# Pooled attention feeding a top-1 mixture of experts: a hold in GpSimd's queue, the pace of three routings and eight weight pieces moved

## The chip, the cores and the metric

The kernel runs on one core of a Trainium2 chip. The metric is the device time of one execution in microseconds (us), as a median over several runs. The core has five engines that each work through a queue of their own in order and wait for each other by semaphores: TensorE (PE; its weight loads are listed as PEld), VectorE (DVE), ScalarE (ACT), GpSimd (POOL) and SyncE (SP), which only issues DMAs here. ACT and GpSimd issue DMAs too.

## What is computed

Attention over keys and values that are averaged in groups of 8 positions, then a mixture of experts in which each row goes to one expert, up to a capacity:

```python
def _attn_ref(q, k, v):              # batch 8, heads 8, seq 576, head_dim 64
    k_p = k.reshape(B, H, Sp, pool, D).mean(axis=3)
    v_p = v.reshape(B, H, Sp, pool, D).mean(axis=3)
    scores = scale * np.matmul(q, k_p.transpose(0, 1, 3, 2))
    scores = scores - np.max(scores, axis=-1, keepdims=True)
    attn = np.exp(scores)
    attn = attn / (np.sum(attn, axis=-1, keepdims=True) + 1e-09)
    return np.matmul(attn, v_p)

def _moe_ref(x, w_gate, w1, w2, capacity):   # x: 4608 rows of 512; 8 experts, hidden 1024
    logits = x @ w_gate
    expert_idx = np.argmax(logits, axis=1)
    ...
    for i in range(N):
        e = expert_idx[i]
        if counts[e] < capacity:
            disp[e, counts[e]] = x[i]
            ...
    h = np.maximum(np.einsum('ecd,edf->ecf', disp, w1), 0.0)
    y = np.einsum('ecf,efd->ecd', h, w2)
    ...
            out[i] = gate_w[i] * y[expert_idx[i], pos[i]]
```

## The kernel before

It has two parts. The attention part takes about the first third of the span, and a loop over tiles of rows of one expert takes the rest. The change touches the attention part alone.

**Units.** The work of the attention is cut into 36 units of 128 rows of queries (line 688): four for each of the 8 batch entries, and one more for each pair of entries, which holds the tails of both. Lines 1029 to 1090 are one Python loop over units n = 0 to 37 that emits the instructions. All engines' orders follow from it, since nothing is scheduled later. In round n unit n gets its scores (`ps`), its maximum (`mx`) and the subtraction (`pt`), unit n+1 its transposed queries (`pq`, copied to `qT` by ACT), and unit n−2 its transposed probabilities (`pp`, copied to `pT` by ACT in two halves), its product with the values (`pa`, line 516, in two halves) and its normalization on DVE (`rz`, `xo`, `lt`, lines 525 to 542). There is one buffer `pa`, so TensorE can begin the next unit's `pa` when `lt` is done.

**Two banks.** The transposes of `pp`, `pq`, `pk` (pooled keys or values), the products `pv` and the routing's sums `po` take turns in two PSUM banks (`bank`, line 247). Each takes the bank of the last but one, and so waits until that one has been read.

**Pooling.** The keys and values of two batch entries (a pair) are summed over 8 positions by trees of three additions on GpSimd (`tree`, lines 365 to 377: L370, L372, L374), six trees a pair. A queue of generators, `gq`, holds these steps, and each round takes some of them (line 1088). `pooled` and `pool` put a pair's trees into the queue. In the rounds of pair 1 a copy to `apart` that reads the newest `mx` (L1019) goes ahead of the fourth pair's trees, so that GpSimd starts them only when DVE has got that far.

**Routing.** When a pair's logits are there, `route` (lines 584 to 686) finds each row's expert and place: `gmx`, `gd` (L598), `gme`, `gmm`, the one-hot `oh` (L614, L617), counts within a block `su` (L621) and `cum` (L628) on DVE, then the sums over partitions and blocks `po` on TensorE (L641), then the places (L644 to L672) on DVE, and at last scatters of row numbers and weights to the table `slots` in DRAM by GpSimd (L679), queued in `sq`. It is a generator, and each `yield` ends a step. A round takes steps of it at several places: one behind `mx`, some behind `pa` (line 1078), and one behind each of three instructions of the normalization. Between L628 and `po` it yields three times when it has more than three groups. `slots` is first filled with defaults by a DMA of the SP queue (L339), which `setup_rows` issues in round 12.

**Early weights.** From round 25 on the first expert's `w1` is loaded into buffers of the pooling. Eight pieces of it are split (L125 on ACT, L126 on GpSimd) into a high part `w1h` and a low part `w1l`, as steps of `gq`: two at the end of each of rounds 26, 27, 30 and 31. `masks` (lines 343 to 347) makes masks from the capacity on DVE in round 27. In round 29 a gather fetches the first rows `xg`, which are transposed in rounds 31 and 32 (`pxe`).

Of the kernel before, what the change touches and what calls it, by code (L numbers as in the profile page):

```python
# [31 lines left out]
def pooled_attn_top1_moe(ctx: ExitStack, tc: tile.TileContext, q, k, v, wg, w1, w2, cap, out):  # L32
# [7 lines left out]
    nc = tc.nc  # L40
# [51 lines left out]
    def gather(dst, ix, src):  # L92
        nc.gpsimd.tensor_sub(guard[:, :, 0:1], ix[:, :, 0:1], ix[:, :, 0:1])  # L93
        for i in range(2):
            nc.gpsimd.indirect_dma_start(out=dst[:, i, :].bitcast(F32), out_offset=None, in_=src,  # L95
                                         in_offset=bass.IndirectOffsetOnAxis(ap=ix[:, i, 0:1], axis=0))
# [65 lines left out]
    with ExitStack() as actx:  # L162
# [10 lines left out]
        def bank(shape, name, dtype=F32):  # L173

            turn[0] ^= 1
            return ptp.tile(shape, dtype, name=name, tag=f"tp{turn[0]}")
# [17 lines left out]
        def load_kv(p):  # L194
            raws[p] = [[early_k if p == 1 and src is k and i == 0 else load_third(src, p, i) for i in range(3)] for src in (k, v)]
# [142 lines left out]
        def setup_rows():  # L338
            nc.sync.dma_start(slots.rearrange("(p c) t -> p c t", p=P), ids[:, 0:NCOL, :])  # L339
            nc.sync.dma_start(xs[NT : NT + 1, :], zrow[0:1])  # L340
            nc.sync.dma_start(capt, cap.bitcast(I32).rearrange("(o c) -> o c", o=1).to_broadcast([P, 2]))
# [11 lines left out]
        apart = ac.tile([P, 1], F32, name="apart")  # L353
# [25 lines left out]
        def red(dst, t):  # L379
            nc.vector.tensor_reduce(out=dst, in_=t.rearrange("p c (j d) -> p c d j", j=POOL), axis=AX.X, op=ALU.add)  # L380

        def pooled(p):

            kps[p] = kvp.tile([P, NR, D], F32, name="kp", tag="kp", bufs=2)
            vps[p] = kvp.tile([P, NR, D], F32, name="vp", tag="vp", bufs=2)
# [181 lines left out]
        first, lgs, rows_out, early = {}, {}, [], {}  # L567

        def flush():
            while rows_out:  # L570
                nc.scalar.dma_start(*rows_out.pop(0))
# [12 lines left out]
        def route(bp, t0, G, blk, tail, prods, sc, count=False, run=None):  # L584
# [7 lines left out]
            f, nb, n = blk  # L592
            bs = slice(f, f + nb * n)
            mx = sm.tile([P, G, 1], F32, name="gmx", tag="gmx")
# [35 lines left out]
            if gn > 3:  # L630
                yield
                yield
                yield
            po = bank([P, 512], "po")[:, 0 : 4 * E].rearrange("p (a e) -> p a e", a=4)
            prods = [x for x in prods if before or x[1] != "c"]
            for n_, (w, x, l, m) in enumerate(prods):
# [60 lines left out]
        rq, hq, aq, dq, sq, gq = [], [], [], [], [], []  # L697
# [26 lines left out]
        def step(q_, n=1):  # L724

            while q_ and n:
                if callable(q_[0]):
                    q_.pop(0)()
                    n -= 1
                elif next(q_[0], 0) == 0:  # L730
                    q_.pop(0)
                else:
                    n -= 1

        def drain(q_):
            while q_:
                step(q_)

        with tc.manual_schedule():
# [26 lines left out]
            nu = len(units)  # L766
            n_start = nu - 3
            early_b = B // 2
            n_early = nu - 11
# [68 lines left out]
            def start_rows():  # L838
                early["x"] = wk.tile([P, 2, DM], F32R, name="xg", tag="xg", bufs=1)
                idp = early["id"]  # L840
                gather(early["x"], idp, xs[0 : early_b * S, :])
# [141 lines left out]
            NPU = 2 * NB + 1  # L983
# [21 lines left out]
            def hooks(n):  # L1005

                p, j = divmod(n, NPU)
                if n == 0:
                    red(vps[0][:, NR - 1 :], raws[0][1][2][:, 2:3])
                    pooled(1)  # L1010
                    pool(1)
                if p == B // 2:
                    return
                if p + 2 < B // 2:
                    if j == (4 if p == 0 else 2):
                        load_kv(p + 2)
                    if j == (7 if p == 0 else 5):
                        if p:
                            nc.gpsimd.tensor_copy(apart, early["mx"][:, 0, 0:1])  # L1019
                        pooled(p + 2)  # L1020
                        pool(p + 2)
                if n == 3 * NB:
                    drain(gq)
                    gq.append(setup_rest())
                    drain(gq)
                    setup_rows()

            for n in range(nu + 2):
                u = units[n] if n < nu else None
                p = units[n - 2] if n > 1 else None  # L1030
                nx = units[n + 1] if n + 1 < nu else None
                new = n and u and u.b != units[n - 1].b
                if new:
                    assert not aq
                    ahead(u.b)
                if n == n_start:
                    start_weights()
                if n == n_early:
                    start_early()
                if n == n_early + 1:  # L1040
                    drain(gq)
                    split_early(0, 2 * KD, nc.gpsimd)
                if n == n_early + 3:
                    start_ids()
                if n == n_early + 4:
                    start_rows()
                if u:
                    u.score(0)
                if p:
                    p.p_t(0)  # L1050
                if u:
                    u.score(1)
                    u.softmax()
                step(aq)
                if p:
                    p.p_t(1)
                if n == nu + 1:
                    for c in range(KF):
                        nc.scalar.copy(wr["h"][:, c], wr[2][:, c])
                if n >= nu:  # L1060
                    hidden(0, n - nu)
                if nx:
                    nx.q_part()
                flush()
                step(aq)
                if n == 1:
                    busy(5)
                    hq.append(prep_v(0))
                    step(hq)
                if u:  # L1070
                    u.exp()
                if p:
                    p.open()
                    p.av(0)
                turns(n)
                if p:
                    p.av(1)
                step(rq, 4 if NPU < n < nu - 8 else 8 if n >= nu - 8 else 0)
                step(dq)
                if p:  # L1080
                    p.norm()
                    r = route_of(p)
                    if r:
                        rq.append(r)
                        if p.b == early_b - 1:
                            rq.append(favourite())
                hooks(n)
                step(gq, 4 if n <= n_early else 0 if n_early + 3 <= n < n_early + 5 else 2)
                step(sq, 2 if n < nu - 10 else 4)
                step(aq)  # L1090
            flush()
# [132 lines left out]
```

## Time and profile before

| | |
|---|---|
| median of 3 runs | 639.11 us (638.94 to 639.9) |
| the profiled execution | 639.53 us, of which its span 637.5 us |
| mean granted TensorE clock | 0.987 |
| attention part | to about 185 us of the span |
| loop over tiles | from about 216 us on |

The profile lists instructions by engine and line, with tiles by the names above (out<-in). A timeline row has the start and the length in us, the engine, line, operation, tiles, shapes, the number of merged instructions, and in brackets the idle time of the engine just before, with what ended it. "pa L516 <- DVE lt L542" in the list of waits is TensorE's wait before `pa` for DVE's `lt`. A windows row has the stretch, its length, the busy time of an engine (with its instructions), the granted clock, the DMA share and GB/s. The granted clock is 1.00 at full speed.

### The profile page before, as it was taken

The numbers are of one execution on the slowest core, as the hardware profiler recorded it, in microseconds if no ns is written. First come the engines' busy times: TensorE is split into PE (matmuls) and PEld (weight loads), VectorE is DVE, ScalarE is ACT, GpSimd is POOL, SyncE is SP. The second block draws the span as 40 slices with busy tenths as digits, with TensorE's granted clock in tenths as the row PEclk, the third lists the DMA queues.
The fourth block names the chain that finished last, engine by engine and source line by source line (L and its number), as shares of the span: only waits on it lengthen the run. The fifth ranks groups of instructions, "written<-read, shape, count | busy, mean of one in ns | idle before, by whom it ended". The sixth has DMA issues, their size and how long they took to land.

```text
span 637.5 us, 14824 instructions
## 1 busy us (share of the span) xinstructions
PE 614.1 (96%) x4249; PEld 554.1 (87%) x4250; DVE 332.5 (52%) x720; ACT 236.3 (37%) x403; POOL 297.4 (47%) x468
## 2 busy tenths in 40 slices
PE   9899999899999999999899999999999999999994
PEld 8889899798889889988789989988899888989983
DVE  4667868777788322268447731326422585323222
ACT  2555576366544211157245511117111472111111
POOL 7799499253743422424435522434434145441344
PEclk9999999799999999999999999999999999999997
DMA  9989953283191610228728640213612181210112
GB/s 325 359 330 323 349 183 122 72 258 101 53 329 53 230 35 33 66 81 309 241 82 308 230 141 33 66 33 120 235 47 66 41 282 36 66 51 19 62 49 66
DMA packets 47084, 93.81 MB, mean 147 GB/s; under 512 B 13392, under 2 KB 23632, under 8 KB 47060
## 3 DMA queue, kind: packets, MB, share of 16 engines
q1 hardware_dynamic: 30836, 60.37, 27.6%
q0 software_dynamic: 11392, 21.57, 11.3%
q10 hardware_dynamic: 4832, 11.56, 4.8%
q8 instruction: 14, 0.23, 0.1%
q14 instruction: 10, 0.08, 0.0%
HBM read 132.97 MB, written 31.27 MB: 258 GB/s over the span
## 4 chain that ended last, share of the span: by engine, by line
PE 60%; DVEq 2%; issue 2%; DVE 1%; POOL 1%; ACT 0%; POOLq 0%; ACTq 0%
PE y L159 30%; PE ph L150 23%; PE ph L1140 4%; PE px L1117 2%; PE ph L1147 1%; DVE w2l L126 0%; POOL out_dram L100 0%; DVE hl L1130 0%; DVEq L1165 0%; DVEq L1164 0%; DVEq L1163 0%; ACT w2h L125 0%; DVEq L1160 0%; DVEq L1159 0%; POOL xg L95 0%
## 5 line engine op out<-in xcount | busy, mean ns | idle before, releaser
L1129 ACT ACTIVATE hh<-ph 128x512 fp32r<-128x512 f32 x60 | 35.8, 598 | 170.1 <-PE ph L150 170.0
L1130 DVE SCALAR_TENSOR_TENSOR hl<-ph,hh 128x512 fp32r<-128x512 f32 x60 | 40.7, 690 | 109.4 <-ACT hh L1129 62.5
L150 PE MATMUL ph<-xh,w1h 128*128 128x256 f32 x480 | 76.5, 282 | 4.6 <-DVE hl L1130 3.9
L150 PE MATMUL ph<-xh,w1l 128*128 128x256 f32 x480 | 75.9, 281 | 0.0
L150 PE MATMUL ph<-xl,w1h 128*128 128x256 f32 x480 | 75.9, 281 | 0.0
L150 PEld LDWEIGHTS ph<-xh,w1h 128*128 128x128 f32 x480 | 65.8, 189 | 6.9 <-DVE hl L1130 4.8
L159 PE MATMUL y<-w2h,hh 128*128 128x512 f32 x280 | 71.7, 398 | 0.0
L95 POOL DMA_INDIRECT xg<-xs,ix x42 | 43.5, 1035 | 58.2 <-PE y L159 50.0
L516 PE MATMUL pa<-vbd,pT 96*128 96x146 f32 (+1 forms) x480 | 67.1, 296 | 3.5 <-DVE lt L542 3.5
L159 PE MATMUL y<-w2h,hl 128*128 128x512 f32 x280 | 69.3, 390 | 0.0
L159 PE MATMUL y<-w2l,hh 128*128 128x512 f32 x280 | 69.2, 389 | 0.0
L150 PEld LDWEIGHTS ph<-xl,w1h 128*128 128x128 f32 x480 | 65.2, 190 | 0.0
L150 PEld LDWEIGHTS ph<-xh,w1l 128*128 128x128 f32 x480 | 64.7, 189 | 0.0
L516 PEld LDWEIGHTS pa<-vbd,pT 96*128 96x128 f32 (+1 forms) x480 | 57.1, 181 | 6.8 <-DVE lt L542 4.5
L159 PEld LDWEIGHTS y<-w2l,hh 128*128 128x128 f32 x280 | 52.6, 188 | 11.1
L159 PEld LDWEIGHTS y<-w2h,hl 128*128 128x128 f32 x280 | 52.6, 188 | 10.9
L100 POOL DMA_INDIRECT out_dram<-zrow,iz x40 | 51.3, 1282 | 16.9 <-issue 14.9
L159 PEld LDWEIGHTS y<-w2h,hh 128*128 128x128 f32 x280 | 49.6, 188 | 9.6 <-ACT hh L125 0.9
L126 DVE TENSOR_TENSOR xl<-px,xh 128x512 fp32r<-128x512 f32 x40 | 25.8, 686 | 60.9 <-ACT xh L125 60.9
L93 POOL TENSOR_TENSOR guard<-ix 128x2 int32<-128x2 int32 x21 | 4.0, 193 | 101.5 <-DVE ix L90 96.8
L503 ACT COPY pT<-pp 96x384 f32<-96x384 f32 x72 | 33.8, 474 | 45.0 <-PE pp L502 44.4
L679 POOL DMA_INDIRECT slots<-pairs,gix x36 | 35.4, 983 | 30.3 <-DVE pairs L672 13.0
(236 smaller groups left out, 1051.8 us busy)
## 6 DMA issues: line engine op xcount, KB each, us to landing
r<-in_moe_w_dram SPq DMA_DIRECT2D x84, 1024.0 KB, 11.1
raw<-in_k_dram SPq DMA_DIRECT2D x12, 768.0 KB, 6.5
raw<-in_v_dram SPq DMA_DIRECT2D x12, 768.0 KB, 10.6
xs<-xo ACTq DMA_DIRECT2D x16, 512.0 KB, 3.1
qblk<-in_q_dram SPq DMA_DIRECT2D x14, 512.0 KB, 7.7
raw<-in_moe_w_dram SPq DMA_DIRECT2D x4, 512.0 KB, 4.8
r<-in_moe_w_dram ACTq DMA_DIRECT2D x2, 1024.0 KB, 6.9
qblk<-in_q_dram SPq DMA_DIRECT2D x4, 256.0 KB, 8.3
```

What stands on the lines that cost most here:

```text
L95: nc.gpsimd.indirect_dma_start(out=dst[:, i, :].bitcast(F32), out_offset=None, in_=src, in_offset=bass.IndirectOffsetOnAxis(ap=ix[:, i, 0: ...
L100: ins = nc.gpsimd.indirect_dma_start(out=out[:, :], out_offset=bass.IndirectOffsetOnAxis(ap=i_, axis=0), in_=src, in_offset=None, bounds_c ...
L126: eng.tensor_sub(lo, src, hi.bitcast(F32))
L150: nc.tensor.matmul(p[:, f2], a[:, c, f * P : (f + 1) * P], b[:, c], start=(f2 == 0 and j == 0 and c == 0), stop=(f2 == 1 and j == 2 and c ...
L159: nc.tensor.matmul(y, a[:, c, i * P : (i + 1) * P], b[:, c], start=(n == 0), stop=(n == 3 * KF - 1))
L503: nc.scalar.copy(self.pT[:, j], pp[0:KC, 0:HC])
L516: nc.tensor.matmul(self.pa[us, j, h0 * XW : (h0 + 2) * XW], self.pT[:, j, c, us], vbd[b % 2][:, cc].rearrange("r a x -> r (a x)"), start=( ...
L679: ins = nc.gpsimd.indirect_dma_start(out=slots[:, :], out_offset=bass.IndirectOffsetOnAxis(ap=ix[:, g, 0:1], axis=0), in_=pairs[:, pr + g0 ...
L1117: nc.tensor.transpose(px[i][:, c], xg[:, i, c * P : (c + 1) * P], identr)
L1129: nc.scalar.activation(hh[s], p, AF.Relu)
L1130: nc.vector.scalar_tensor_tensor(out=hl[s], in0=p, scalar=0.0, in1=hh[s].bitcast(F32), op0=ALU.max, op1=ALU.subtract)
L1140: nc.tensor.matmul(ph[f], a[:, c, r], b[:, c, fs], start=(j == 0 and c == 0), stop=(j == 2 and c == KD - 1))
```

## The change

There are four edits. `route` yields a fourth time ahead of `po`. The hold goes from round 14, ahead of `pooled(3)`, to round 12, ahead of `setup_rows`, and `pooled(3)` and `pool(3)` go from round 14 to round 13. The steps of a routing behind `pa` are eight instead of four up to round 13, which concerns the first routing alone. And the eight `w1` pieces are taken by rounds 26 (two at the end), 27 and 28 (three each: one behind the first `pp`, one behind the second, one at the end).

```diff
@@ route
             if gn > 3:
                 yield
                 yield
                 yield
+                yield
             po = bank([P, 512], "po")[:, 0 : 4 * E].rearrange("p (a e) -> p a e", a=4)
@@ hooks
-                    if j == (7 if p == 0 else 5):
-                        if p:
-                            nc.gpsimd.tensor_copy(apart, early["mx"][:, 0, 0:1])
+                    if j == (7 if p == 0 else 4):
                         pooled(p + 2)
                         pool(p + 2)
                 if n == 3 * NB:
                     drain(gq)
                     gq.append(setup_rest())
                     drain(gq)
+                    nc.gpsimd.tensor_copy(apart, early["mx"][:, 0, 0:1])
                     setup_rows()
@@ the loop over rounds
+                more = 1 if n_early + 1 < n < n_early + 4 else 0
                 if u:
                     u.score(0)
                 if p:
                     p.p_t(0)
+                step(gq, more)
                 if u:
                     u.score(1)
                     u.softmax()
                 step(aq)
                 if p:
                     p.p_t(1)
+                step(gq, more)
@@
-                step(rq, 4 if NPU < n < nu - 8 else 8 if n >= nu - 8 else 0)
+                step(rq, 8 if n < 2 * NPU - 4 or n >= nu - 8 else 4)
@@
-                step(gq, 4 if n <= n_early else 0 if n_early + 3 <= n < n_early + 5 else 2)
+                step(gq, 4 if n <= n_early else 2 if n == n_early + 1 else 1)
```

Here NB is 4, NPU is 9, nu is 36 and n_early is 25. From `route` on the changed kernel's line numbers are one to three higher.

How the instructions move is shown at three places. On TensorE in round 12, the first routing's sums (`po`) against the transposes of probabilities (`pp`) and queries (`pq`):

```order
 L479 MATMUL ps<-kbs_146,qT 128x144 x2
+L642 MATMUL po<-su,matr 128x16
+L642 MATMUL po<-oh_180,matr 128x8
+L642 MATMUL po<-su,matr 128x24
+L642 MATMUL po<-oh_180,matr 128x8
+L642 MATMUL po<-su,matr 128x8 x2
+L642 MATMUL po<-oh_180,matr 128x8
 L502 MATMUL pp<-identr,pt 96x128 x3
 L462 MATMUL pq<-identr,qtail 128x128 x4
```

The sums stood behind the second half of `pa` at the end of the round, and now stand between the scores and the second `pp`. The third routing's sums move to the same place of round 30.

On DVE at the same place, from the one-hot `oh` to the subtraction `pt` of round 12, first before:

```order
L614 TENSOR_TENSOR oh_180<-cw,gmm 128x2x32
L525 TENSOR_SCALAR rz<-pa 128x8
L617 TENSOR_TENSOR oh_180<-cw,gmm 128x8
L527 RECIPROCAL rz<-rz 128x8
L621 TENSOR_REDUCE su<-oh_180 128x80
L541 TENSOR_TENSOR xo<-pa,rz 128x2x256
L542 TENSOR_TENSOR lt<-pa,rz 128x2x32
L628 TENSOR_REDUCE oh_181<-oh_180 128x8
L486 TENSOR_REDUCE mx<-ps 128x8
L491 TENSOR_TENSOR pt<-ps,mx 128x4x2x72
```

and in the changed kernel:

```order
L617 TENSOR_TENSOR oh_180<-cw,gmm 128x8
L621 TENSOR_REDUCE su<-oh_180 128x80
L628 TENSOR_REDUCE oh_181<-oh_180 128x8
L525 TENSOR_SCALAR rz<-pa 128x8
L527 RECIPROCAL rz<-rz 128x8
L541 TENSOR_TENSOR xo<-pa,rz 128x2x256
L542 TENSOR_TENSOR lt<-pa,rz 128x2x32
L486 TENSOR_REDUCE mx<-ps 128x8
L645 TENSOR_TENSOR gps<-su,po 128x64
L647 SCALAR_TENSOR_TENSOR gps<-po,oh_180 128x8
L491 TENSOR_TENSOR pt<-ps,mx 128x4x2x72
```

The counts no longer alternate with the normalization, and the two readers of `po` (L644 and L646 before) stand between `mx` and `pt` instead of behind the round's `vbd`.

On ACT from the end of round 26 to that of round 28, in the changed kernel, the casts `w1h` are the pieces:

```order
 L125 CAST w1h<-raw 128x512 x2
+L503 COPY pT<-pp 96x384
+L125 CAST w1h<-raw 128x512
+L503 COPY pT<-pp 96x384
+L125 CAST w1h<-raw 128x512
+L463 COPY qT<-pq 128x512
+L571 DMA xs<-xo 128x1024
+L494 ACTIVATE pt<-pt 128x576
+L125 CAST w1h<-raw 128x512
+L503 COPY pT<-pp 96x384
+L125 CAST w1h<-raw 128x512
+L503 COPY pT<-pp 96x384
```

Behind these rows come the second piece of round 28, `qT`, `pt`, four copies `kbs` and then the last piece, ahead of round 29's first `pT`. Before, two pieces stood behind `pt` in each of rounds 26, 27, 30 and 31. GpSimd's subtractions `w1l` move along: all six later ones now stand directly behind one scatter, ahead of the gather. On GpSimd the hold (`apart<-mx`) moves from behind the first routing's first two scatters to ahead of them. The order of scatters and trees behind it is the same. On SP nothing moves.

## The prediction

> **What bounds the kernel now.** I read the page first, then TensorE's waits, the granted clock in windows, and the timeline of each engine where TensorE waits.
>
> ```profile
> span 637.5 us, 14824 instructions
> PE 614.1 (96%) x4249; PEld 554.1 (87%) x4250; DVE 332.5 (52%) x720; ACT 236.3 (37%) x403; POOL 297.4 (47%) x468
> ```
>
> TensorE is busy 96% of the span, in one order of instructions, so a microsecond that it waits is a microsecond of the kernel, and work on other engines counts only where TensorE waits for it. The change lies in the attention part (units 11 to 33), where these are the waits that it can touch (us in total, times, longest):
>
> ```profile
> PE pa L516 <- DVE lt L542: 3.5, 4, 2.1
> PE po L641 <- DVE su L621: 1.9, 2, 1.2
> PE pq L462 <- ACT pT L503: 0.3, 1, 0.3
> ```
>
> These are small, but two of them cost more than their length. The windows below show PE's busy time, the granted clock (the second number after the busy time), and DMA:
>
> ```profile
> 112.21:115.62 3.41, 2.28 (x19) 1.00 0.21 72
> 115.62:122.45 6.83, 6.83 (x37) 0.50 0.00 0
> 153.17:156.58 3.41, 2.70 (x24) 1.00 0.57 214
> 156.58:159.99 3.41, 3.41 (x17) 0.50 0.02 7
> ```
>
> After the 2.1 us wait (unit 21) the clock stands at 0.50 for 6.83 us, and after a 0.7 us wait (unit 30; 1.9 less the longest, 1.2) for 3.41 us. TensorE is busy all that time, so at half clock it loses up to 3.4 and 1.7 us. In both cases the stretch ahead held a wait and the tiny matmuls of a routing's sums.
>
> **The first routing, eight steps a unit.** Before, it stands so:
>
> ```profile
> 70.36 0.62 PE L462 MATMUL pq<-identr,qtail 128*128 128x128 f32 x4
> 71.39 1.02 PE L516 MATMUL pa<-vbd,pT 96*128 96x146 f32 x6 [0.41 <-DVE lt L542]
> ...
> 74.26 0.27 PE L641 MATMUL po<-su,matr 128*128 128x16 f32 x1
> ...
> 75.13 0.71 PE L476 MATMUL ps<-kbs,qT 128*64 128x144 f32 x8
> ```
>
> The sums (po) take 0.87 us, 74.26 to 75.13. The order shows that they now stand ahead of the second transposes of unit 12, and that DVE makes oh and su in one go and reads po behind unit 12's maximum (mx). What this takes on DVE is read from unit 29, where the same steps already run in one go:
>
> ```profile
> 69.50 0.23 DVE L614 TENSOR_TENSOR oh<-cw,gmm 128x64 fp32r<-128x64 f32 x1
> ...
> 154.28 0.23 DVE L614 TENSOR_TENSOR oh<-cw,gmm 128x64 fp32r<-128x64 f32 x1
> ...
> 154.54 0.69 DVE L621 TENSOR_REDUCE su<-oh 128x80 fp32r<-128x320 f32 x1
> ...
> 156.44 0.21 DVE L542 TENSOR_TENSOR lt<-pa,rz 128x64 f32<-128x64 f32 x1
> ...
> 156.70 0.16 DVE L646 SCALAR_TENSOR_TENSOR gps<-po,oh 128x8 f32<-128x8 f32 x1
> 158.57 0.76 DVE L486 TENSOR_REDUCE mx<-ps 128x8 f32<-128x576 f32 x1 [1.71 <-PE ps L479]
> ```
>
> There su ends 0.95 and lt 2.37 us after L614 starts. From 69.50 that gives su at 70.45 and lt at 71.87. TensorE reaches po at about 70.0 and waits 0.4. It is done with po at 71.3 and wants pq at 71.65. But the transposes, pq and po take turns in two PSUM banks, and with po one place further up pq gets po's bank. That is free when DVE has read it, with two short instructions (L644, L646) that now queue behind mx: 71.87, plus 0.76, plus twice some 0.15, is 72.9. So pq waits about 1.2. The old wait of 0.4 at pa goes, since lt is long done. The routing's rest then comes as one block ahead of unit 12's rz:
>
> ```profile
> 73.79 0.94 DVE L442 TENSOR_TENSOR vbd<-pv,mk 96x768 f32<-96x768 f32 x1
> ...
> 163.32 1.11 DVE L662 TENSOR_SCALAR ghi<-gpos 128x9 f32<-128x9 f32 x1
> ...
> 165.08 0.11 DVE L525 TENSOR_SCALAR rz<-pa 128x8 f32<-128x8 f32 x1
> ...
> 166.07 0.21 DVE L542 TENSOR_TENSOR lt<-pa,rz 128x64 f32<-128x64 f32 x1
> 77.68 1.66 PE L516 MATMUL pa<-vbd,pT 96*128 96x146 f32 x12
> ```
>
> From L662 to rz is 1.76 us, of which L662 was held for about 0.9; with L655 and L658 ahead of it the block is some 1.3, and rz to the end of lt 1.2. TensorE's pv comes 1.9 later, so vbd ends at 76.6 and lt at 79.1; pa of unit 13 is wanted at 77.68 plus 1.05, and waits 0.4. In sum this edit costs 0.4 + 1.2 + 0.4 − 0.4 = 1.6 us of waits. Windows of 3.41 us around it now hold a wait and the tiny matmuls together, as the two windows above did, so I expect the clock to halve there for two windows: 3.4 us, with 0 and 1.7 as the other values.
>
> **The hold of the fourth pair's sums.** GpSimd is to start the trees two units earlier. But what stands ahead of them in its queue?
>
> ```profile
> slots<-ids SPq DMA_DIRECT2D x1, 288.0 KB, 12.2
> 66.88 0.43 SPq L339 DMA_DIRECT2D slots<-ids x1
> 79.98 1.17 POOL L679 DMA_INDIRECT slots<-pairs,gix  x1 [9.01 <-DVE rz L527]
> ...
> 82.41 0.20 POOL L1019 COPY apart<-mx 128x1 f32<-128x1 f32 x1
> ```
>
> Two scatters of the first routing come first. They write slots, which the SP queue fills by a DMA issued at 66.88 that lands 12.2 us later, at 79.1, in both kernels. In before the routing's pairs came at about the same time, so the trace does not tell which of the two released the scatter; in the changed kernel the DMA does. The copy that holds was not waited for (it ran right behind the second scatter). So the trees start some 0.2 us earlier, not two units. Taken alone this edit is worth nothing, and its other bound (no such wait) is a rival below.
>
> What then becomes of unit 21?
>
> ```profile
> 107.83 1.59 DVE L598 TENSOR_TENSOR gd<-lg,gmx 128x72 f32<-128x72 f32 x1
> ...
> 109.98 1.69 DVE L614 TENSOR_TENSOR oh<-cw,gmm 128x64 fp32r<-128x64 f32 x1
> 110.59 0.62 PE L462 MATMUL pq<-identr,qtail 128*128 128x128 f32 x4
> 113.34 1.01 PE L516 MATMUL pa<-vbd,pT 96*128 96x146 f32 x6 [2.13 <-DVE lt L542]
> 111.66 0.62 POOL L374 TENSOR_TENSOR vp<-t 128x192 f32<-128x192 f32 x1
> ```
>
> In the second routing L598 and L614 took 1.6 and 1.7 us, against 0.23 for L614 in unit 12: each ran while GpSimd summed a tree. The last of these (L374) ends at 112.3, and by the last paragraph near 112 in both kernels. If TensorE and DVE come here 1.6 later, the trees hide under that: of the 2.1 us wait about 0.5 is left and the window may stay full. If they come 5.0 later (waits and the slow clock of unit 12), L598 starts behind the last tree, and nothing is left. By either way the 2.1 + 3.4 us that unit 21 lost go, or nearly.
>
> **A step more before the sums.** It moves po of the third routing from the end of unit 29 to unit 30, behind four score matmuls and three transposes, and there su is 0.7 us done. The wait and the slow window go: 0.7 + 1.7. The bank of po is again what pq takes next, but here mx runs before po ends, so I take 0 (up to 1.2 as in unit 12). The last pair's first routing keeps its place on TensorE and its 1.2 us wait. In the second routing the step only lets the normalization's rz go ahead of one short instruction, which costs nothing: TensorE needs lt, and lt comes no later.
>
> **The w1 pieces.**
>
> ```profile
> 145.98 1.12 ACT L125 CAST w1h<-raw 128x512 fp32r<-128x512 f32 x2
> ...
> 151.24 0.47 ACT L503 COPY pT<-pp 96x384 f32<-96x384 f32 x1
> 151.80 0.62 PE L462 MATMUL pq<-identr,qblk 128*128 128x128 f32 x4
> 166.34 1.01 PE L516 MATMUL pa<-vbd,pT 96*128 96x146 f32 x6 [0.75 <-DVE lt L542]
> 144.19 1.00 POOL L679 DMA_INDIRECT slots<-pairs,gix  x1
> 145.28 0.14 DVE L344 CAST capf<-capt 128x1 f32<-128x1 int32 x1
> ```
>
> Two pieces at the end of unit 27 held ACT's first pT copy of unit 28, which is the 0.3 us wait at pq; with one there it goes. But in unit 28 ACT now has three pieces and four kbs copies. The last piece (0.56 of the 1.12) stands ahead of unit 29's first pT copy, which moves from 151.24 to 151.7 and ends at 152.2. The bank is wanted for pq at 151.80 less the 0.3 won, so TensorE waits 0.7. Units 30 and 31 lose their pieces: L662 is not held by GpSimd any more (0.9), and of the 0.75 wait about 0.2 stays, a gain of 0.55. GpSimd's work ends sooner, so SP may issue the next weights' loads sooner; they are awaited long after, so nothing comes of it.
>
> **The sum**, against the profiled execution's 639.53 us (2.0 of it outside its span, unchanged). Removed: 0.4 + (2.1 + 3.4) + 0.3 + (0.7 + 1.7) + 0.55 = 9.15. Added: 0.4 + 1.2 + 0.4 + 3.4 + 0.7 = 6.1. Net 3.05: 636.5, and by the median (639.11, 0.4 below that execution) **636.1 us**.
>
> **The rivals.**
>
> *The clock stays up.* The waits around unit 12 are 1.2 and shorter, and one row speaks for it: the 1.2 us wait at unit 33 (the longest in po's row) was followed by no slow window. Then 3.4 less is added, 0.5 stays at unit 21, and the time is 636.1 − 3.4 + 0.5 = 633.2; with one slow window instead of two, about 634.5. The Trainium skill (TensorE: Matmul & The Clock Gate, "Why this matters for your kernels") says that gaps up to about 3 us between matmuls do no harm. By that rule this rival would be sure; the trace disagrees, with half clock after waits of 2.1 and of 0.7 us. Chance 0.32.
>
> *The trees do move.* If the pairs, not the DMA, released the first scatter at 79.98, the trees end some 3 us earlier and unit 21 loses nothing even with the clock up at unit 12: 633.2 − 0.5 = 632.7. Against it stands the landing at 79.1. Chance 0.07.
>
> *GpSimd's pieces hold the masks: slower.* In unit 27 a piece now starts on GpSimd at 145.2, where the scatter of 144.19 ends, and five more follow. DVE's cast L344 starts at 145.28 and two mask instructions follow, with unit 27's rz behind them and TensorE's pa behind that. L662, a small TENSOR_SCALAR, was held by a piece until it ended. If all three are held in turn, by about 1.1 each, pa of unit 28 waits about 3.1, and a wait like that halves the clock as unit 21's did: 3.1 + 3.4 = 6.5, so 642.6. If the cast alone is held, it is 1.1 and 637.2. It decides with the first of the three: 0.14 us long, or over 1. For it stands L662. The Trainium skill (SBUF — State Buffer, "Who interferes with whom") says that casts and tensor_scalar may use the port that GpSimd shares, and that an instruction with at most one SBUF input outside such a mode does not; no row here shows a cast beside a piece. Chance 0.08 for all three, 0.10 for the cast alone.
>
> **How the numbers follow.** The forecast (one slow stretch left, at unit 12) has 0.43; its own range is 635 to 637.2. The clock staying up has 0.32, moved trees 0.07, the cast alone 0.10, all three masks 0.08. From 632.8 to 638.0 leaves out the slower rival, and most of the moved trees. About 0.2%, 1.3 us, is what a measurement can tell: faster means below 637.8. That holds for the first three cases and most of the fourth, less something for a slow window that a shifted order brings elsewhere: 0.85; within 0.2% 0.08; slower 0.07.
>
> **What would show it.** Right: pq of unit 12 waits for DVE about 1.2; the first scatter still starts near 80 and the trees still end near 112; no 2.1 us wait before unit 21's pa; no half clock near 157; pq of unit 29 waits for ACT 0.7. Wrong: trees ending by 109, a cast L344 of over 1 us, or half clock after unit 28.

## The result, and the profile after

The changed kernel is slower: 644.79 us in the median (642.03 to 650.64, 11 runs) against 639.11 (632.1 to 643.63, 11 runs) for the kernel before; the ratio is 1.013 (95% interval 1.0086 to 1.0174). The profiled execution took 644.79 us. This is the outcome that the prediction kept as its slower rival, at 0.08, with 642.6 us.

The page of the changed kernel begins with

```profile
span 643.1 us, 14828 instructions
PE 616.5 (96%) x4249; PEld 555.7 (86%) x4250; DVE 336.5 (52%) x720; ACT 236.7 (37%) x403; POOL 298.7 (46%) x468
```

and these are the three rows of TensorE's waits that answer to those of before (us in total, times, longest):

```profile
PE pa L516 <- DVE lt L542: 7.6, 4, 5.3
PE pq L462 <- PE pp L502: 1.3, 2, 0.9
PE po L642 <- DVE su L621: 1.2, 1, 1.2
```

The waits for su fell from 1.9 to 1.2, as forecast. The waits before pa grew from 3.5 to 7.6, and one of 5.3 is new. The windows show what stands around the waits of unit 21 (the first two rows) and unit 28 (the last two); the columns are as before:

```profile
113.10:116.51 3.41, 1.84 (x16) 1.00 0.34 116
116.52:123.35 6.83, 6.83 (x37) 0.50 0.00 0
150.65:154.07 3.42, 0.00 (x0) 1.00 0.00 0
154.07:160.90 6.83, 6.54 (x28) 0.50 0.00 0
```

Unit 21 has kept most of its wait (1.86 of 2.13 us) and all of its half clock. From 150.65 to 154.07 TensorE did nothing at all, and for the next 6.83 us it ran at half clock. Where the time came in is read from the start of the same matmul in the two timelines:

| TensorE reaches | before | after | later by |
|---|---|---|---|
| the second scores of unit 12 (L479) | 69.54 | 69.98 | 0.4 |
| the first scores of unit 13 (L476) | 75.13 | 76.06 | 0.9 |
| pa of unit 21 | 113.34 | 114.67 | 1.3 |
| pa of unit 28 | 148.02 | 154.36 | 6.3 |
| po behind the last pair's wait for su | 178.94 | 185.68 | 6.7 |
| the end of the span | 637.5 | 643.1 | 5.6 |

Of the 6.7 us, 5.0 come in at one place, pa of unit 28. The timelines of GpSimd, DVE and TensorE say why:

```profile
145.50 0.98 POOL L680 DMA_INDIRECT slots<-pairs,gix  x1 [0.15 <-issue]
146.51 6.16 POOL L126 TENSOR_TENSOR w1l<-raw,w1h 128x512 fp32r<-128x512 f32 x5
...
146.58 0.14 DVE L344 CAST capf<-capt 128x1 f32<-128x1 int32 x1
146.76 6.08 DVE L346 TENSOR_SCALAR mkeep<-spos,capf 128x288 int32<-128x288 f32 x1
152.77 0.36 DVE L346 TENSOR_SCALAR mdrop<-spos,capf 128x288 int32<-128x288 f32 x1
153.06 0.15 DVE L525 TENSOR_SCALAR rz<-pa 128x8 f32<-128x8 f32 x1
...
154.36 1.83 PE L516 MATMUL pa<-vbd,pT 96*128 96x146 f32 x6 [5.34 <-DVE lt L542]
```

Five pieces run on GpSimd without a gap from 146.51 to 152.67. DVE's first mask begins 0.25 us into them and ends 0.17 us behind them: 6.08 us. The second mask takes 0.36, much as both did before (0.37). Behind the masks stand rz, xo and lt in DVE's queue, and TensorE waits for lt. In the kernel before, GpSimd was idle there:

```profile
145.46 0.37 DVE L346 TENSOR_SCALAR mkeep<-spos,capf 128x288 int32<-128x288 f32 x1
...
146.67 2.48 POOL L126 TENSOR_TENSOR w1l<-raw,w1h 128x512 fp32r<-128x512 f32 x2 [1.49 <-ACT w1h L125]
```

The masks were done by 146.1, and the first piece came at 146.67.

Of the prediction's signs of being wrong, half clock after unit 28 has come. Of its signs of being right, pq of unit 12 waits and unit 30 has no half clock of its own, but unit 21's wait stands, and pq of unit 29 doesn't wait. The first scatter and the last tree stand a little later than the 80 and 112 that it named. The first row below is from the profile's list of DMAs: the fill of `slots`, with the time from issue to landing at its end.

```profile
slots<-ids SPq DMA_DIRECT2D x1, 288.0 KB, 12.8
67.73 0.42 SPq L339 DMA_DIRECT2D slots<-ids  x1
72.63 0.63 PE L462 MATMUL pq<-identr,qtail 128*128 128x128 f32 x4 [0.93 <-PE pp L502]
81.48 1.17 POOL L680 DMA_INDIRECT slots<-pairs,gix  x1 [8.74 <-DVE rz L527]
112.99 0.62 POOL L374 TENSOR_TENSOR vp<-t 128x192 f32<-128x192 f32 x1
114.67 1.02 PE L516 MATMUL pa<-vbd,pT 96*128 96x146 f32 x6 [1.86 <-DVE lt L542]
166.87 0.63 PE L462 MATMUL pq<-identr,qtail 128*128 128x128 f32 x4 [0.34 <-PE pp L502]
```

The wait at pq is 0.93 (forecast 1.2). The prediction had the fill land at 79.1 in both kernels. Here it lands at 80.5 (67.73 plus 12.8), the scatter starts at 81.48, 1.5 us later than before, and the trees end at 113.6 instead of 112.3. So unit 21's routing, whose L598 came 1.7 us later (109.49), met them again.

### The profile page after: what moved, and what is told of

It is laid out like the page before. It is cut to its first block, busy times and chain, and to the rows that moved or that the text cites. A ratio compares the mean times of both kernels' runs of the same rounds, so it can differ in the third digit from the quotient of the medians.

```text
span 643.1 us, 14828 instructions
## 1 busy us (share of the span) xinstructions
PE 616.5 (96%) x4249; PEld 555.7 (86%) x4250; DVE 336.5 (52%) x720; ACT 236.7 (37%) x403; POOL 298.7 (46%) x468
## 4 chain that ended last, share of the span: by engine, by line
PE 59%; DVEq 2%; issue 1%; DVE 1%; POOL 1%; ACT 0%; POOLq 0%; ACTq 0%
PE y L159 30%; PE ph L150 23%; PE ph L1143 4%; PE px L1120 2%; PE ph L1150 1%; POOL out_dram L100 0%; DVE hl L1133 0%; DVE w2l L126 0%; ACT w2h L125 0%; DVEq L1167 0%; DVEq L1168 0%; DVEq L1166 0%; DVEq L1163 0%; DVEq L1162 0%; POOL xg L95 0%
## 5 line engine op out<-in xcount | busy, mean ns | idle before, releaser
L516 PE MATMUL pa<-vbd,pT 96*128 96x146 f32 (+1 forms) x480 | 68.8, 301 | 7.7 <-DVE lt L542 7.6
L516 PEld LDWEIGHTS pa<-vbd,pT 96*128 96x128 f32 (+1 forms) x480 | 58.4, 184 | 11.6 <-DVE lt L542 9.1
```

The source lines that it names most:

```text
L516: nc.tensor.matmul(self.pa[us, j, h0 * XW : (h0 + 2) * XW], self.pT[:, j, c, us], vbd[b % 2][:, cc].rearrange("r a x -> r (a x)"), start=( ...
```

## The experiments

The sixteen runs below fall into four groups, each on one chip. The kernel before took 638.8, 643.7, 643.7 and 638.4 us in them, so only ratios within a group compare closely. A ratio is to the kernel before in the same group, with its 95% interval; a gain or loss in us is worked out from it, where the text doesn't say "by the medians".

### Which edit is it?

**The pieces back.** The changed kernel with the step counts of `gq` as before, so that the pieces go back to rounds 26, 27, 30 and 31:

```diff
-                more = 1 if n_early + 1 < n < n_early + 4 else 0
...
-                step(gq, more)
...
-                step(gq, more)
...
-                step(gq, 4 if n <= n_early else 2 if n == n_early + 1 else 1)
+                step(gq, 4 if n <= n_early else 0 if n_early + 3 <= n < n_early + 5 else 2)
```

> The changed kernel with the eight w1 pieces back in rounds 26, 27, 30 and 31; the three other edits stay. Theory (the masks are held): the loss is all in the pieces. The first mask (L346) takes 0.37 us again instead of 6.08, unit 28's pa loses its 5.3 us wait, and the 6.83 us at half clock behind it (3.4 us lost) go: 644.8 - 5.3 - 3.4 = 636.1, plus 0.3 (the pq of unit 28) and some 0.5 (L662 held again): near 637, and 2 us below the kernel before. Rival (the eight steps and the hold cost it: waits and half clock between units 12 and 21): the time stays within 1.5 us of the changed kernel's, 643 to 646. Second rival (the pieces hid something else that was won): back at the kernel before, 639.

Measured: 638.12 us, ratio 1.0001 (0.9974 to 1.0028). The 5.3 us wait is gone. The loss goes with the pieces; the 2 us that the three other edits were to gain aren't there.

**The pieces alone.** The opposite edit, on the kernel before.

> The kernel before with the move of the eight w1 pieces alone. Theory (the masks are held): unit 27's first L346 takes about 6 us, pa of unit 28 waits about 5.3, and a stretch at half clock follows: 639.1 + 5.3 + 3.4 - 0.85 (pq of unit 28, pa of unit 31), less up to 2.4 if unit 30's own wait and half clock go with it: 645 to 647. Rival (the loss needs the other edits, since only with them do masks and pieces meet): L346 0.37 us and 639.

Measured: 644.97 us, ratio 1.0113 (1.0074 to 1.0153), by the same mask:

```profile
146.04 6.17 POOL L126 TENSOR_TENSOR w1l<-raw,w1h 128x512 fp32r<-128x512 f32 x5
...
146.28 6.10 DVE L346 TENSOR_SCALAR mkeep<-spos,capf 128x288 int32<-128x288 f32 x1
...
153.90 1.83 PE L516 MATMUL pa<-vbd,pT 96*128 96x146 f32 x6 [5.36 <-DVE lt L542]
```

This edit alone does as much harm as the whole change.

**The masks elsewhere.** The changed kernel, with the masks in the round where batch entry 5 begins (22), in which GpSimd has no pieces:

```diff
-                if b == LAST - 1:
+                if b == LAST - 2:
                     dq.append(masks)
```

> The changed kernel with the masks in round 22 instead of 27, where GpSimd has no work; the pieces stay where the change has them. Theory (only the masks are held): both L346 take 0.37 us, pa of unit 28 waits under 1 us, no half clock near 154: 644.8 - 5.3 - 3.4 = 636.1, with 0.7 more if the last piece on ACT now delays the pq of unit 29. Rival (whatever DVE's tensor_scalar stands there is held, next rz of unit 27, L525, which stood right behind the masks): L525 takes 5 us, pa of unit 28 waits as long as now, 644 to 645.

Measured: 638.47 us, ratio 1.0004 (0.9978 to 1.0029). The time is about 2 us above the theory's 636.1 to 636.8, but its mechanism is there. The pieces still run as five in a row, and no DVE instruction is held by them. (A scatter ran beside the masks here, from 125.21 to 126.19, and didn't hold them.) pq of unit 29 waits for ACT, as forecast, 0.6 us:

```profile
125.30 0.37 DVE L346 TENSOR_SCALAR mkeep<-spos,capf 128x288 int32<-128x288 f32 x1
...
153.53 0.66 PE L462 MATMUL pq<-identr,qblk 128*128 128x128 f32 x4 [0.61 <-ACT pT L503]
```

So it is neither the pieces nor their new rounds by themselves but their meeting with the masks. The rival (rz held in their place) falls.

**The change once more**, on the chip of the last group.

> The changed kernel again, on the chip of the three others. Theory: 1.0 to 1.5% above the kernel before, L346 about 6 us, pa of unit 28 waits 5.3 us. Rival (the loss hangs on the chip): within 0.5% of the kernel before.

Measured: 645.74 us, ratio 1.013 (1.0081 to 1.018); the first mask took 6.10 and pa of unit 28 waited 5.35. The loss doesn't hang on the chip.

### When does a held instruction get its turn?

**A memset between the pieces.** The changed kernel with a GpSimd instruction of one element per partition ahead of each piece:

```diff
+            def piece(hi, lo, src, eng):
+                nc.gpsimd.memset(apart, 0.0)
+                split(hi, lo, src, eng)
...
-                    gq.append(partial(split, w1h[:, c, fs], w1l[:, c, fs], early["w1"][c][:, fs], eng))
+                    gq.append(partial(piece, w1h[:, c, fs], w1l[:, c, fs], early["w1"][c][:, fs], eng))
```

> The changed kernel with a memset of one element per partition on GpSimd ahead of each w1 piece. Theory A (a held DVE instruction gets its turn as soon as GpSimd changes instruction, and the five pieces were one unbroken run only because nothing stood between them): L346 takes 1.2 to 1.5 us instead of 6.08. Theory B (it gets its turn only when GpSimd has nothing ready to start): L346 still takes about 6 us.

Measured, in one profiled execution: the first mask took longer still.

```profile
149.74 7.04 DVE L346 TENSOR_SCALAR mkeep<-spos,capf 128x288 int32<-128x288 f32 x1
...
150.28 1.30 POOL L126 TENSOR_TENSOR w1l<-raw,w1h 128x512 fp32r<-128x512 f32 x1
151.49 0.12 POOL L825 MEMSET apart<- 128x1 f32 x1
151.54 1.28 POOL L126 TENSOR_TENSOR w1l<-raw,w1h 128x512 fp32r<-128x512 f32 x1
...
155.31 1.27 POOL L126 TENSOR_TENSOR w1l<-raw,w1h 128x512 fp32r<-128x512 f32 x1
```

It ended at 156.78, behind the last of the five pieces (156.58). Theory A falls: a change of instruction opens nothing as long as the next one is ready.

**A copy that waits for the piece.** The same, with `nc.gpsimd.tensor_copy(apart, lo[:, 0:1].bitcast(F32))` behind each piece, which reads what the piece wrote.

> The changed kernel with a GpSimd copy of one element per partition behind each w1 piece that reads what the piece wrote, so that GpSimd waits for the piece to be finished, as the second and third addition of a tree wait for the one before. Theory A and theory B alike: L346 takes 1.2 to 1.5 us, since a real gap of some 0.1 us opens behind each piece, and pa of unit 28 waits under 1 us. Rival: the hold lasts as long as GpSimd has work at all: about 6 us.

Measured, in one profiled execution:

```profile
151.40 0.37 DVE L346 TENSOR_SCALAR mkeep<-spos,capf 128x288 int32<-128x288 f32 x1
151.70 2.05 DVE L346 TENSOR_SCALAR mdrop<-spos,capf 128x288 int32<-128x288 f32 x1
...
152.30 1.28 POOL L126 TENSOR_TENSOR w1l<-raw,w1h 128x512 fp32r<-128x512 f32 x1
153.64 0.18 POOL L826 COPY apart<-w1l 128x1 f32<-128x1 f32 x1
153.78 1.26 POOL L126 TENSOR_TENSOR w1l<-raw,w1h 128x512 fp32r<-128x512 f32 x1
```

Here the first mask came ahead of the pieces. The second began beside a scatter (151.26 to 152.26) and was held on through one piece. It ended at 153.75, at the gap behind that piece, with five more to come. It took longer than the forecast 1.2 to 1.5 us, since its hold began in the scatter already: alone it would have ended near 152.07, before the piece started. pa waits 1.3 at most (forecast: under 1).

The routings show the same without any added instruction. In the first profile of the change L614, 0.23 us when alone, was held from within a scatter and through the addition behind it, and ended at 113.00, at the gap of 0.08 us ahead of the next addition (112.99, shown above), which reads that addition's sum:

```profile
110.84 1.04 POOL L680 DMA_INDIRECT slots<-pairs,gix  x1
111.31 1.69 DVE L614 TENSOR_TENSOR oh<-cw,gmm 128x64 fp32r<-128x64 f32 x1
111.90 1.01 POOL L372 TENSOR_TENSOR t<-t 128x384 f32<-128x384 f32 x1
```

Together: a held instruction gets its turn in a gap in which GpSimd waits for itself, here 0.06 and 0.08 us long, and not between two instructions that follow each other at once. The Trainium skill (SBUF — State Buffer, "Who interferes with whom") says that whoever issues first has the shared ports for the whole instruction; the 6.08 us, for five instructions of 1.23, show that here one may have to wait for a whole row of them. (The times of these two kernels, 658.1 and 653.5 us by one run each, hold extra GpSimd work and aren't used.)

### What are the other edits worth?

**The fourth yield alone.**

> The kernel before with the fourth yield alone. Theory: the third routing's sums come behind unit 30's scores and transposes, the 0.7 us wait for su and the 3.41 us at half clock go, and nothing comes instead: 639.1 - 0.7 - 1.7 = 636.7. Rival (the stretch at half clock comes from something else there, or moves): 638.4 to 639.

Measured: 638.66 us, ratio 1.0012 (0.9986 to 1.0039). The wait for su at unit 30 is gone, and pq waits there instead, for the bank:

```profile
157.83 0.63 PE L462 MATMUL pq<-identr,qtail 128*128 128x128 f32 x4 [0.59 <-PE pp L502]
```

0.7 goes and 0.6 comes. The forecast 636.7 isn't reached, no gain is measured, and the half clock at unit 30, which I counted at 1.7, isn't a fixed cost (below).

**The eight steps alone.**

> The kernel before with eight steps a unit in the first routing alone. Theory: the sums reach TensorE ahead of unit 12's second transposes, pq waits about 0.9 for the bank, and all four scatters of the first routing's start stand ahead of the trees, which still end late: unit 21 keeps its 2 us wait. Half clock falls near unit 12, near unit 21 or at both, by where the 3.41 us windows lie: 0 to 5 us above the kernel before. Rival (the pace costs nothing, since the waits only change places): within 1 us of it.

Measured: 646.21 us, ratio 1.0047 (1.0025 to 1.0069): 3 us lost. po of the first routing waits 1.29 for su, pq doesn't wait, and half clock stands at 71.05 for 3.41 us. The theory's wait at unit 21 isn't there. Two more stretches of 3.41 us at half clock, at 132.49 and 180.27, and a wait of 2.1 us at 130.92 stand further on; the first group's traces have no such wait there (see below), so not all of the 3 us is shown to be the eight steps' own.

**The hold alone.**

> The kernel before with the hold moved from round 14 to round 12 and the fourth pair's trees queued in round 13, alone. Theory (with four steps a unit the first scatter is queued behind four additions of the trees, so that GpSimd has work from 72 on instead of waiting for the pairs and the fill until 80): the trees end near 107 instead of 112.3, L598 and L614 of the second routing take some 0.25 us, unit 21's 2.1 us wait and its 6.83 us at half clock go: 4 to 5.5 us below the kernel before. Rival (as the prediction put it, the edit alone is worth nothing: the scatters stand ahead and start near 80 whatever the hold): no difference.

Measured: 642.55 us, ratio 0.9983 (0.9963 to 1.0002). The order differs from that of the changed kernel: with four steps a unit, four additions of the trees stand ahead of the first scatter.

```profile
72.44 0.18 POOL L1024 COPY apart<-mx 128x1 f32<-128x1 f32 x1 [1.43 <-DVE mx L486]
72.59 1.80 POOL L370 TENSOR_TENSOR t<-raw 128x768 f32<-128x768 f32 x1
...
81.35 1.17 POOL L679 DMA_INDIRECT slots<-pairs,gix  x1 [3.39 <-DVE rz L527]
...
106.24 0.59 POOL L374 TENSOR_TENSOR vp<-t 128x192 f32<-128x192 f32 x1
```

The trees end at 106.8, and unit 21 has no wait and no half clock. Of the 5.5 us that this should save 1.1 shows (−0.1 to 2.4 by the interval). A new wait stands further on, with half clock from 129.31 to 136.14 behind it:

```profile
128.00 0.54 PE L502 MATMUL pp<-identr,pt 128*96 128x128 f32 x3 [2.06 <-ACT kbs L417]
126.23 1.71 ACT L417 COPY kbs<-pk 64x320 f32<-64x320 f32 x4 [1.78 <-PE ps L479]
126.31 0.17 DVE L525 TENSOR_SCALAR rz<-pa 128x8 f32<-128x8 f32 x1 [2.07 <-PE ps L479]
```

ACT and DVE both start again near 126.3, though pa, which rz reads, ended at 124.6. What held both, the trace doesn't tell.

**The hold with the masks in round 22**, otherwise the kernel before.

> The kernel before with the hold in round 12 and the masks in round 22, nothing else. Theory (the masks only push the steps of unit 23 and 24 to another time, and the stall near 126 needs its exact meeting): no 2.1 us wait of pp for kbs, no half clock behind it, and the whole gain of the hold: 2.5 to 5.5 us below the kernel before. Rival (the stall stays): 1 us below it, as with the hold alone.

Measured: 634.95 us, ratio 0.9954 (0.993 to 0.9978). That wait isn't there, and the two edits together win 2.9 us. The masks' move was not measured alone.

**The kernel before, profiled again**, on the same chip.

> The kernel before, profiled again. Theory (the 2.1 us wait of pp for kbs near 126 to 130 comes with the hold, since the second routing is no longer held and ACT and DVE arrive there at another time): not in this trace, and unit 21's 2.1 us wait is. Rival (it belongs to the chip): both waits are in this trace.

Measured: unit 21 waits 1.5 us, with 10.24 us at half clock from 113.56 on; no wait of pp near 128. But this was another chip than that of the hold alone. On the chips of the second and third groups all five kernels with the masks in round 27 show the wait of 2.1 to 2.2 us, that with the eight steps alone among them, which has no hold in round 12; the three with the masks in round 22 don't. So the hold isn't its cause by itself. The kernel before was not profiled on those chips, and how much of the hold's gain this wait took stays open.

**An early fill.** The changed kernel, masks in round 22, with the fill of `slots` issued in round 11 ahead of the fourth pair's loads:

```diff
-            nc.sync.dma_start(slots.rearrange("(p c) t -> p c t", p=P), ids[:, 0:NCOL, :])
...
+                        if p:
+                            nc.sync.dma_start(slots.rearrange("(p c) t -> p c t", p=P), ids[:, 0:NCOL, :])
                         load_kv(p + 2)
```

> The changed kernel with the masks in round 22 and with the fill of slots issued by SP in round 11, ahead of the fourth pair's loads, instead of round 12, behind them. Theory (the fill's DMA, not the hold, released the first scatter): the fill lands before 70, the first scatter starts with its pairs near 77.8 instead of 81.5, the trees end near 109.5 instead of 113.6, L598 of the second routing takes some 0.25 us instead of 1.26, unit 21's wait (1.5 to 1.9) and its 6.83 us at half clock go: 3 to 5 us below the kernel with masks early alone (638.5): 634 to 635.5. Rival (the hold's or the pairs' time decides, the landing is chance): the scatter stays within 1 us of 81.5 and the time at 638.5.

Measured: 646.4 us, ratio 1.0028 (0.9998 to 1.0059). A miss: in this execution the clock stood at half from 72.34 to 82.58, so the pairs themselves came only at 79.5, the scatter at 79.80, the trees at 111.9. Unit 21's routing came later still and met none, as my forecast had it for the change itself. The early fill does show what releases the scatter: here it starts 0.3 us behind the last of its pairs, while in the first profile of the change it started 3.9 us behind them and 0.95 behind the fill's landing. There the fill decided, as the prediction said.

**Four steps again** on top of it.

> As the last kernel, but with four steps a unit in the first routing, as before. By my steps for the eight steps (1.2 at pq and 0.4 at lt added, 0.4 at pa saved, and half clock near unit 12 in those executions whose windows fall so) this is 1 to 4 us below the last kernel: 632 to 634. Rival: with four steps the pairs come about a round later, the scatters too, and the trees run into the second routing again: the time of the last kernel or 2 us above it.

Measured: 641.67 us, ratio 0.9965 (0.9938 to 0.9991). Against the last kernel, on the same chip, the four steps save 4.7 us by the medians. The trace has no half clock near 72, trees done at 105.3, and no wait at unit 21.

**Without the early fill.**

> The changed kernel with the masks in round 22 and four steps a unit in the first routing, as before; the fill of slots stays in round 12. Theory (the hold works as soon as the eight steps are gone, whenever the fill comes): as the kernel with the early fill as well, 0.3 to 0.8% below the kernel before. Rival (the early fill was needed: the first scatter waits in the midst of the trees for the fill to land, and they run into the second routing): unit 21 waits again, no better than the kernel before.

Measured: 642.11 us, ratio 0.997 (0.9949 to 0.9992). The early fill isn't needed.

**Without the moved pieces.**

> The fourth yield, the hold and the early fill, with four steps a unit, the pieces in rounds 26, 27, 30 and 31 and the masks in round 27, both as before. Theory (the move of the pieces is worth next to nothing even where it does no harm: 0.6 lost at the pq of unit 29, 0.3 and 0.6 won at the pq of unit 28 and the pa of unit 31): within 1 us of the kernel that has the pieces moved and the masks early. Rival (the move saves what it was costed at or more): 1 to 2 us slower than that one.

Measured: 639.79 us, ratio 0.9945 (0.9922 to 0.9969), against 0.9965 with the pieces moved. The two ratios come from different chips and their intervals overlap; nothing speaks for the move.

**The best one**: the fourth yield, the hold and the early fill, four steps, the pieces as before, the masks in round 22.

> The fourth yield, the hold, the early fill and the masks in round 22, with four steps a unit and the pieces in rounds 26, 27, 30 and 31 as before. Theory: as the kernel with the masks in round 27 (0.55% below the kernel before) or up to 2 us better, if the stall near 126 goes. Rival (masks in round 22 cost something of their own, as in the kernel with the pieces moved that was 0.2% slower than the one without): 0.3% below the kernel before.

Measured: 632.75 us, ratio 0.9927 (0.9894 to 0.996), 4.7 us below the kernel before, and 13 below the changed kernel in the same group, by the medians. TensorE's windows from unit 20 to unit 30 have lost their half clock (3.41 us of it are left, at 173.1):

```profile
109.10:116.00 6.90, 6.90 (x64) 1.00 0.63 229
116.00:126.00 10.00, 9.88 (x80) 1.00 0.38 122
126.00:160.00 34.00, 32.47 (x281) 1.00 0.50 151
```

## Why the prediction was wrong

**The step that failed is the one on the w1 pieces.** It costed the move by ACT's copies alone (0.3 and 0.55 won, 0.7 lost) and left what GpSimd's half of the pieces does to DVE to a rival. ACT's terms were about right: pq of unit 29 waited 0.6 as soon as unit 28 did not, and the 0.75 at unit 31's pa is gone. But the masks met the pieces, in both profiles of the change and in that of the pieces alone: 5.3 us of wait at pa of unit 28, and 6.83 us at half clock behind it in the first profile of the change. The rows that should have raised that chance stood in the prediction: L662 held by a piece, L598 and L614 held by trees (and L614 by a scatter ahead of the addition), and the order, which put six pieces where the masks start; five of them ran in a row. Nothing in them spoke for the masks going free.

**The rival had the right mechanism and a wrong place and size.** I took three instructions held by 1.1 each, and a test by the cast L344. The cast wasn't held (0.14). The first mask was, once, for the whole row of pieces, and the others not. L662 in the kernel before couldn't tell this: it had met the last of two pieces, so the end of a piece and the end of the row were the same. That pa waited 5.3 and not 3.1 is the mis-sized term; the half clock behind it was counted at 3.4 and stood for 6.83 us at 0.50, which loses up to 3.4.

**The sum, term by term.** By the rows of the first profile of the change, 4.1 us went: 0.4 at pa of unit 12, 0.3 at pq of unit 28, 0.7 and up to 1.7 at unit 30, 0.75 at pa of unit 31, and 0.3 of unit 21's wait. And 10.0 came: 0.9 at pq of unit 12, 0.3 at that of unit 30, 5.3 and up to 3.4 at pa of unit 28. The 0.4 at po, the 0.4 at pa of unit 13 and the 0.7 at pq of unit 29 didn't come. Net that is 5.9; the span grew by 5.6. The 8.7 us behind the masks, for which the sum had nothing, turned its sign. A second term failed too: of the 5.5 us that unit 21 was to save only 0.3 were saved. The 3.4 us for half clock at unit 12 weren't spent, so these two misses differ by 1.8 only.

**The eight steps: an either-or taken for one of its sides.** Forecast were waits of 1.6 us net, half clock for two windows near unit 12, and then a free unit 21. In the first profile of the change there is no half clock at unit 12. In the second execution of the same kernel there is:

```profile
73.08:79.91 6.83, 6.83 (x37) 0.50 1.01 385
```

and there L598 of unit 21 took 0.24 and nothing waited, just as forecast. So my forecast is one of two ways in which this kernel runs. In the other the trees and the routing shift together, and unit 21 pays nearly as before; the rival for it (the clock stays up, 0.32) left only 0.5 us there, where 1.86 and 6.83 us at half clock stood. All eight traces of kernels with the eight steps agree: six have half clock near unit 12 (3.41 to 10.24 us) and no wait at unit 21, and two have none and wait 1.5 and 1.9 us there. (One of the six, the pieces back, has 3.41 us at half clock at 120.56 all the same.)

The windows tell the two apart. The changes of the clock in each trace lie whole multiples of 3.41 us from each other, so the ends of the windows near 72 can be worked out. In the two traces without half clock at unit 12, an end falls 0.5 and 0.7 us before the wait there (at pq; with the eight steps alone, at po) is over, so the wait is split between two windows. In the other six the end falls between 0.1 us before the end of the wait and 1.1 us behind it, so one window holds all but 0.1 us of it. No experiment moved the windows; this agrees with the eight traces and isn't tested beyond them. At unit 30 the windows don't tell: in the second profile of the kernel before one window, 154.52 to 157.93, holds the whole wait of 0.71 us and the sums, and no half clock follows.

**The hold: right in the change, wrong alone.** With the eight steps the scatters stand ahead of the trees and wait for the fill; the trees don't start earlier, as said. "Taken alone this edit is worth nothing" was wrong: with four steps it puts four additions ahead of the scatters, the trees end at 106.8, and together with the masks out of round 27 it wins 2.9 us. I costed the edit in the order that the other edit had made, and didn't ask for the order without it.

**The yield: the term taken as 0 was 0.6.** The bank's wait at pq, with my bounds 0 and 1.2, was 0.59 alone and 0.34 in the first profile of the change. Alone it nearly spends the 0.7.

**Half clock is not a constant of a place.** I charged 1.7 us at unit 30 and 3.4 at unit 21 from one execution. I also read that both stretches ahead held the tiny matmuls of a routing's sums. For unit 21 that was misread: the stretch ended at 115.62, and po begins at 116.78, at half clock already. And the stretch ahead of unit 28's half clock held no matmul at all. So the tiny matmuls aren't shown to matter. The second profile of the kernel before shows 10.24 us at unit 21 and none at unit 30, though the 0.71 us wait for su stands there in both. Of the eleven runs of the changed kernel those at a mean clock of 0.986 or 0.983 took 642.0 to 644.8 us, and those at 0.977 took 647.2 to 650.6.

## What to carry to other kernels

Before work is moved on GpSimd, list what DVE runs beside it: a DVE instruction of the kinds that were held here (the masks, L598, L614, L662) waits for the end of the unbroken row, so a bundle of pieces can cost its whole length and not that of one piece. Where two queues must meet, put the DVE instruction into a round without such a row. A wait of GpSimd for itself between pieces lets the DVE instruction in too, but what that is worth in time was not measured. Cost each edit in the order that it makes alone as well as in the order that all make together, and take half clock behind a wait as a chance, not as a sum.

## What the runs showed of the hardware that was not expected

- A one-element memset of GpSimd between two pieces doesn't let DVE in (7.04 us over five pieces); a gap of 0.06 or 0.08 us, in which GpSimd waits for its own result, does.
- The cast of one column from int32 (L344) ran beside a piece in 0.14 us; the mask of 288 columns that reads SBUF and writes int32 (L346) was held.
- Two executions of one kernel put half clock at different places (units 12 and 28, or units 21 and 28). The windows of 3.41 us lie elsewhere in each (an end near 72 falls at 72.15 in the first profile of the change, 13 windows ahead of the 116.52 shown above, and at 73.08 in the second).
- On the chips of the second and third groups the five kernels with moved pieces show a wait of 2.3 to 2.4 us at pxe for which the trace names nothing, and the five with the masks in round 27 the wait of 2.1 to 2.2 us at pp for kbs, with a stop of ACT and DVE ahead of it where it was read (near 126, the hold alone). Neither was settled, and the chips of the other two groups show neither.
